# Rebuilding the prologue of a fused layer-norm, attention and GLU kernel: V projected early, statistics over two engines, the reciprocal root on GpSimd

## Chip, cores, metric

One core of a Trainium2 chip. The metric is the device time of one execution in microseconds (us). A program is run several times, in turn with the kernel before on the same chip; medians are quoted, and ratios with a 95% interval. **A ratio is the mean time of one kernel's fast runs over that of the other's of the same rounds**, so it is not quite the ratio of the medians. "Faster" needs 2%.

Engines: PE (matmuls; PEld is its loading of weights), ACT (ScalarE), DVE (VectorE), POOL (GpSimd), SP (issues DMAs). In the traces below ACT, DVE and POOL each work through one queue in order, which will matter (in run u, POOL's copy that waited 7.76 us for a load held up all that stood behind it). An eviction copies a result out of PSUM, where matmuls leave it in banks. The granted clock is the share of full speed that PE was given (1.00 is full). In a chain of waits, "issue" is time in which an engine waited for nothing that the profile shows, and POOLq is POOL's sequencer. `L260` is line 260 of the kernel; the two kernels' line numbers differ.

## The reference, cut to what matters

```python
x: [1, 2048, 640] bf16;  wqkv: [640, 1920];  wo: [640, 640];  w_gate, w_up: [640, 1728];  w_down: [1728, 640]
xn = (x - mean(x)) / sqrt(var(x) + 1e-5)                 # over the 640 columns
q, k, v = split of xn @ wqkv;   32 heads of 20
s = concat_heads(softmax(q @ k.T * 20**-0.5) @ v) @ wo
g = silu((sigmoid(xn @ w_gate) * (xn @ w_up)) @ w_down)
out = x + s * g
```

## The kernel before

Three stages. The **prologue** normalizes x in four quarters of 512 rows (4 tiles of 128 rows each), transposes it, and projects K (all quarters) and q (the first 512) of heads 0-3. It ends with the first score matmul, because the scores need q, which needs a bound made from the maximum over all of K. The **loop** runs attention and the GLU interleaved. Its order of issue on PE, ACT and DVE is made at build time by a small list scheduler with a model of durations and some tuned constants. Most exponentials are ACT's (from PSUM); for up to four key tiles in each block of 512 queries they are DVE's: an eviction to integers for each head, then four passes over the tile, after which PE needs four matmuls a head instead of one. The **tail** projects the last outputs.

The prologue (statistics, root, scaling, transposes, K):

```python
for c in range(NQC):                                  # 4 quarters
    for i in range(4):                                # DVE: statistics of 128 rows
        for h in range(2):
            nc.vector.bn_stats(out=stats[:, h, :], in_=xt[:, i, h * HD:(h + 1) * HD])
        nc.vector.bn_aggr(out=mv[:, i, :], in_=stats)
    nc.scalar.activation(out=rstd, in_=mv[:, :, 1:2], func=ACT.Sqrt, bias=eps_t, scale=1.0)
    if c == NQC - 1:
        exp_act(eps_t, eps_t)                         # loads the table of Exp
    nc.vector.reciprocal(out=rstd, in_=rstd)
    nc.vector.scalar_tensor_tensor(out=nb, in0=mv[:, :, 0:1], scalar=-1.0, in1=rstd, ...)
    for i in range(4):                                # DVE: the scalings
        nc.vector.tensor_scalar(out=xn[:, i, :], in0=xt[:, i, :], scalar1=rstd[:, i, :], scalar2=nb[:, i, :], ...)
    for kd in range(KD):                              # PE transposes, ACT copies
        ... nc.tensor.transpose(...) ; nc.scalar.copy(out=xnT[:, kd, c * 512:(c + 1) * 512], in_=tp)
    k_mm(psk, 0, c); k_evac(psk, 0, c, on_act=True)
    k_max(0, c)                                       # DVE, reads the evicted K
    # c == 0: q_mm, q_abs
q_bound(psq, 0, aq0); q_evac(psq, qts[0])
# ... (POOL fills constants before all this; cut)
```

The loop (V of heads 0-7 is an item of it; the q of later units takes an Abs on ACT; the last GLU tile has 64 of 128 columns):

```python
URGENT, ROUNDS, HOLD, SLACK, LEAD, LAG, D_LAST, D_LAST_END = 0.15, 4, 0.0, 0.1, 20.0, -5.0, 20, 0
items = [mk_v(0, t, 0.0) for t in VT]
def ab(): aqs[(u, c)] = q_abs(st["ps"])               # ACT Abs from PSUM, 16 times
# mk_gu: 5 matmuls for gate, 5 for up, for every tile, the half one too
# ...
```

The prologue's instructions are ordered by the compiler's tile scheduler, not in program order, on every engine.

## Time and profile before

| kernel before | us |
|---|---|
| median of its 3 first runs (883.49 to 885.87) | 885.81 |
| the profiled run | 879.89, span 878.0 |
| prologue, to the first score matmul | 36.5 |
| first score to the end of the last exponential | 818.3 |

The page's busy times, share of the span, and numbers of instructions:

```profile
PE 825.9 (94%) x7177; PEld 292.7 (33%) x7232; DVE 712.7 (81%) x1234; ACT 823.1 (94%) x1064; POOL 92.1 (10%) x134
```

By windows, prologue and loop (each engine's busy us and, in brackets, its instructions; then granted PE clock, DMA share, GB/s):

```profile
core 0: us, PE busy (x) PEld busy (x) DVE busy (x) ACT busy (x) POOL busy (x), PEclk, DMA share, GB/s
0.00:36.47 36.47, 16.58 (x106) 8.97 (x109) 25.85 (x80) 16.97 (x32) 8.96 (x30) 0.95 0.57 156
36.47:854.80 818.33, 792.31 (x6962) 275.86 (x7018) 676.55 (x1135) 806.13 (x1032) 74.39 (x94) 1.00 0.24 66
```

In the prologue DVE is the busiest engine; in the loop ACT is busy 98.5% and PE 96.8% of the time.

Some pieces of the chain of waits through the prologue (start, length, what):

```profile
11.43 1.41 DVE xn L261 x4
14.35 2.73 DVE xn L261 x4
...
30.27 2.55 ACT xnT L269 x5
...
32.86 0.39 PE psk L144
...
33.27 0.70 ACT kT_81 L152
...
33.99 0.70 DVE mk_223 L160
```

DVE's scalings are the first link; the last quarter's copies, K, eviction and maximum are the last. The second quarter's four scalings took twice the first's; POOL was filling constants then.

### The profile page before, as it was taken

The page shows a single profiled execution, that of the slowest core. Times are in us where ns is not written, and L with a number is a line of the kernel's source. Part 1 is how long each engine was busy: PE and PEld are TensorE (multiplying, and loading weights), DVE is VectorE, ACT ScalarE, POOL GpSimd, SP SyncE. Part 2 cuts the span into 40 slices and gives each one's busy share as a digit, 9 for nine tenths or more (in the row PEclk, how much of TensorE's full clock was granted, in tenths as well). Part 3 has the DMA queues.
Part 4 walks back from the last instruction along what each step waited for, and adds up shares of the span by engine and source line. Part 5 has one row for each costly group of instructions (what it writes and reads, how often), then busy time and mean ns, then how long its engine had stood idle before and what let it go on. Part 6 is the DMA issues. An engine that isn't in the chain of part 4 may idle for free.

```text
span 878.0 us, 18830 instructions
## 1 busy us (share of the span) xinstructions
PE 825.9 (94%) x7177; PEld 292.7 (33%) x7232; DVE 712.7 (81%) x1234; ACT 823.1 (94%) x1064; POOL 92.1 (10%) x134
## 2 busy tenths in 40 slices
PE   3699999999999999999999999999999999988897
PEld 2333223333333323333333333334333233322233
DVE  8558988988877798678878878989888868988884
ACT  4699999999999999999999999999999999999990
POOL 4010000111000000010000000002000000002233
PEclk9899999999999999999999999999999999999998
DMA  7401212122222132212113222211122211241332
GB/s 208 144 11 47 58 46 66 50 59 59 71 67 77 35 82 79 59 47 75 41 48 82 71 78 72 82 51 48 44 71 72 66 43 47 75 133 54 102 105 98
DMA packets 90361, 61.98 MB, mean 71 GB/s; under 512 B 32024, under 2 KB 83784, under 8 KB 90272
## 3 DMA queue, kind: packets, MB, share of 16 engines
q1 hardware_dynamic: 88832, 59.15, 24.2%
q10 hardware_dynamic: 1440, 1.64, 0.6%
q8 instruction: 56, 0.92, 0.4%
q14 instruction: 33, 0.27, 0.1%
HBM read 45.91 MB, written 12.39 MB: 66 GB/s over the span
## 4 chain that ended last, share of the span: by engine, by line
PE 41%; ACT 39%; DVE 12%; issue 7%; DMA 1%; POOLq 0%; SPq 0%; DVEq 0%; POOL 0%; ACTq 0%
PE oacc L780 11%; PE scA_449 L740 6%; PE scA_448 L740 6%; DVE pb L825 4%; PE bk_452 L538 4%; DVE iv L1044 4%; PE bk_451 L561 2%; PE bk_450 L538 2%; ACT tnh L87 2%; PE bk_452 L402 1%; DVE stats L249 1%; PE bk_450 L561 1%; PE bk_452 L561 1%; PE bk_451 L538 1%; ACT aq L174 1%
## 5 line engine op out<-in xcount | busy, mean ns | idle before, releaser
L825 DVE TENSOR_SCALAR pb<-iv 128x2048 int16<-128x2048 int16 x424 | 291.7, 708 | 2.5
L1044 DVE TENSOR_SCALAR iv<-bk_452 128x512 int16<-128x512 f32 x165 | 112.8, 684 | 35.5 <-PE bk_452 L740 35.0
L1044 DVE TENSOR_SCALAR iv<-bk_450 128x512 int16<-128x512 f32 x138 | 94.1, 682 | 31.2 <-PE bk_450 L740 30.9
L810 POOL TENSOR_TENSOR on_bf<-on,rl 128x512 bf16<-128x512 f32 x30 | 40.1, 1337 | 608.5 <-DMA rl<-rd 431.1
L1044 DVE TENSOR_SCALAR iv<-bk_451 128x512 int16<-128x512 f32 x121 | 82.5, 682 | 23.5 <-PE bk_451 L740 23.4
L538 PE MATMUL bk_452<-xnT,wgu 128*128 128x512 bf16 (+1 forms) x274 | 80.7, 383 | 1.7 <-issue 1.0
L740 PEld LDWEIGHTS <-kT_81 32*128 32x128 bf16 x1024 | 38.2, 91 | 131.0 <-issue 127.8
L780 PE MATMUL oacc<-pb,vs_86 128*21 128x512 bf16 x648 | 80.3, 382 | 1.3 <-DVE pb L825 1.0
L740 PEld LDWEIGHTS <-kT_82 32*128 32x128 bf16 x1024 | 39.8, 91 | 117.2 <-issue 109.2
L780 PE MATMUL oacc<-pb,vs_85 128*21 128x512 bf16 x624 | 70.6, 381 | 0.5 <-issue 0.3
L538 PEld LDWEIGHTS <-wgu 128*128 128x128 bf16 (+1 forms) x560 | 43.0, 98 | 70.0 <-issue 44.6
L561 PEld LDWEIGHTS <-hT 128*128 128x128 bf16 x448 | 35.4, 97 | 43.7 <-issue 34.2
L780 PEld LDWEIGHTS <-v_84 128*21 128x21 bf16 x1024 | 30.5, 90 | 45.5 <-issue 36.3
L780 PEld LDWEIGHTS <-v_83 128*21 128x21 bf16 x1024 | 29.1, 90 | 43.4 <-issue 33.4
L538 PE MATMUL bk_450<-xnT,wgu 128*128 128x512 bf16 x140 | 40.5, 382 | 0.8 <-issue 0.6
L780 PE MATMUL oacc<-pb,v_84 128*21 128x512 bf16 x216 | 33.7, 382 | 1.7 <-DVE pb L825 1.5
L561 PE MATMUL bk_451<-wd,hT 128*128 128x320 bf16 (+1 forms) x168 | 33.4, 303 | 0.0
L538 PE MATMUL bk_451<-xnT,wgu 128*128 128x512 bf16 (+1 forms) x99 | 29.2, 383 | 1.1 <-issue 0.6
L780 PE MATMUL oacc<-pb,v_83 128*21 128x512 bf16 x208 | 30.2, 383 | 0.0
L740 PE MATMUL scA_448<-q_94,kT_81 32*128 32x512 bf16 x134 | 27.3, 386 | 1.4 <-DVE q_94 L181 0.8
L780 PEld LDWEIGHTS <-vs_86 128*21 128x21 bf16 x648 | 21.5, 91 | 21.3 <-issue 14.4
L740 PE MATMUL scA_449<-q_95,kT_82 32*128 32x512 bf16 x133 | 26.4, 383 | 1.3 <-ACT pt_5196 L87 0.5
(1834 smaller groups left out, 2377.8 us busy)
## 6 DMA issues: line engine op xcount, KB each, us to landing
wgu<-in_B_w_gate_dram SPq DMA_DIRECT2D x24, 320.0 KB
wgu<-in_B_w_up_dram SPq DMA_DIRECT2D x24, 320.0 KB
rl<-rd SPq DMA_DIRECT2D x120, 64.0 KB
gq_dram<-gqs SPq DMA_DIRECT2D x32, 160.0 KB
ob<-gq_dram SPq DMA_DIRECT2D x12, 320.0 KB
wd<-in_B_w_down_dram SPq DMA_DIRECT2D x1, 2080.0 KB
oU<-on_bf SPq DMA_DIRECT2D x104, 20.0 KB
ob<-in_A_x_dram SPq DMA_DIRECT2D x12, 160.0 KB
```

What stands on the lines that cost most here:

```text
L87: return nc.scalar.add_instruction(mybir.InstActivation(func=func, name=nc.get_next_instruction_name(), engine=ENG.Activation, ins=[nc.sca ...
L174: nc.scalar.activation(out=aq, in_=ps, func=ACT.Abs)
L249: nc.vector.bn_stats(out=stats[:, h, :], in_=xt[:, i, h * HD:(h + 1) * HD])
L402: nc.tensor.matmul(st["ps"][0:UC, :], lhsT=wus[u][:, kd, i, :], rhs=xnT[:, kd, c * QC:(c + 1) * QC], start=(kd == 0), stop=(kd == KD - 1))
L538: nc.tensor.matmul(st[key][0:fs, :], lhsT=w[:, i, kd, ko * P:ko * P + fs], rhs=xnT[:, kd, c * QC:(c + 1) * QC], start=(kd == 0), stop=(kd ...
L561: nc.tensor.matmul(st["ps"][:, 0:HD], lhsT=hT[0:fsz[kf], kf, t4 * P:(t4 + 1) * P], rhs=wd[0:fsz[kf], kf, h * HD:(h + 1) * HD], start=(kf = ...
L740: nc.tensor.matmul(dst, lhsT=kTs[(b // NQC) % 2][32 * j:32 * j + 32, kt * P:(kt + 1) * P], rhs=qts[b % 3][32 * j:32 * j + 32, :], start=Tr ...
L780: nc.tensor.matmul(oacc[32 * j:32 * j + DH + 1, :], lhsT=lhsT, rhs=u["src"], start=first, stop=last, tile_position=(0, 32 * j), skip_group ...
L810: nc.gpsimd.tensor_tensor(out=on_bf, in0=on, in1=rl, op=ALU.mult)
L825: nc.vector.tensor_scalar(out=pb[:, k, :, :].bitcast(I16), in0=iv, scalar1=0.25, scalar2=cst, op0=ALU.mult, op1=ALU.add)
L1044: nc.vector.tensor_scalar(out=d["iv"][:, j, :], in0=bank[bk], scalar1=I_OFF, scalar2=I_LOW, op0=ALU.add, op1=ALU.max)
```

## The change

Its intent: shorten the prologue, use its idle PE for V of heads 0-7, and relieve ACT and PE in the loop.

```diff
-URGENT, ROUNDS, HOLD, ... D_LAST, D_LAST_END = 0.15, 4, 0.0, 0.1, 20.0, -5.0, 20, 0
+URGENT, ROUNDS, HOLD, ... D_LAST, D_LAST_END = 0.1, 4, 0.3, 0.1, 20.0, -5.0, 16, 8
@@ prologue (cut to its core) @@
+def stats_act(c, i):                       # one tile of four in each quarter: ACT
+    nc.scalar.activation(out=sq, in_=xts[c][:, i, :], func=ACT.Copy, scale=1.0 / D, accum_out=mvs[c][:, i, 0:1])
+    nc.scalar.mul(out=nm, in_=mvs[c][:, i, 0:1], mul=-root)
+    nc.scalar.activation(out=sq, in_=xts[c][:, i, :], func=ACT.Square, bias=nm, scale=root, accum_out=mvs[c][:, i, 1:2])
-    nc.scalar.activation(out=rstd, in_=mv[:, :, 1:2], func=ACT.Sqrt, bias=eps_t, scale=1.0)
-    nc.vector.reciprocal(out=rstd, in_=rstd)
+def rstd_of(c):                            # POOL: (var + eps) ** -0.5
+    nc.gpsimd.tensor_scalar(out=rstd, in0=mvs[c][:, :, 1:2], scalar1=1e-5, scalar2=0.0, op0=ALU.add, op1=ALU.add)
+    nc.gpsimd.tensor_tensor(out=rstd, in0=rstd, in1=mhalf, op=ALU.pow)
-    k_max(0, c)
+    k_max(0, c, psk)                       # from PSUM; one K bank instead of two
+    project_v(c)                           # 20 matmuls, ACT evicts
+exp_act(eps_t, eps_t)                      # the only table load, at the start
+for i in range(3): stats_dve(0, i)
+stats_act(0, 3)
+for c in range(NQC):
+    rstd_of(c)
+    if c == 0: spread_wst(0, wst0)
+    if c == 1: constants()                 # POOL's fillings, before: ahead of the loop
+    if c == 3: more_constants()
+    if c + 1 < NQC:
+        stats_act(c + 1, 3)
+        stats_dve(c + 1, 0)
+    scale(c)                               # nb, scalings, transposes; in the last quarter DVE makes 2 of 5 copies
+    if c + 1 < NQC:
+        for i in (1, 2): stats_dve(c + 1, i)
+    project_k(c); project_v(c)
@@ loop @@
-items = [mk_v(0, t, 0.0) for t in VT]
+items = []
-            aqs[(u, c)] = q_abs(st["ps"])                                   # ACT
+            nc.vector.scalar_tensor_tensor(out=aqs[(u, c)][0:UC, :], in0=st["q"], scalar=-1.0,
+                                           in1=st["q"], op0=ALU.mult, op1=ALU.max)
+        # last GLU tile: 64 gate and 64 up columns side by side in one tile, 5 matmuls instead of 10
```

The loads of x are also spread over two queues by tile instead of by quarter, and the loop's order of issue is made anew.

More of the change, by code (lines that the diff above doesn't have):

```diff
@@ L30 @@
 UC = UH * DH
-URGENT, ROUNDS, HOLD, SLACK, LEAD, LAG, D_LAST, D_LAST_END = 0.15, 4, 0.0, 0.1, 20.0, -5.0, 20, 0
+URGENT, ROUNDS, HOLD, SLACK, LEAD, LAG, D_LAST, D_LAST_END = 0.1, 4, 0.3, 0.1, 20.0, -5.0, 16, 8
 D_ORD, M_ORD, WAIT3, FALL = 0, 1, 0.0, 1
@@ L116 @@
     eps_t = const.tile([P, 1], FP32, name="eps_t")
+    mhalf = const.tile([P, 4, 1], FP32, name="mhalf")
     qts = [persist.tile([P, QC], BF16, name=f"q{i}") for i in range(3)]
@@ L124, with load_wst @@
     wqkv_v = A_wqkv.rearrange("(kd p) (t c) -> p kd t c", p=P, t=3)
-    def load_wqk(g):
+    def load_wst(g):
         st = wk.tile([P, KD, 2, GC], BF16, tag="wst", bufs=1, name="wst")
@@ L129, in load_wqk, with spread_wst @@
             nc.sync.dma_start(out=st[:, :, t, :], in_=wqkv_v[:, :, t, g * GC:(g + 1) * GC])
+        return st
+    def spread_wst(g, st):
         nc.gpsimd.tensor_copy(out=wqks[g % 2][:, :, :, 1:1 + DH],
@@ L154, in k_evac, with k_max @@
             nc.vector.tensor_scalar(out=dst, in0=ps, scalar1=ones_r[:, 0:1], scalar2=None, op0=ALU.add)
-    def k_max(g, c):
+    def k_max(g, c, src=None):
         if not mk_n.setdefault(g, []):
@@ L159, in k_max @@
         mk_n[g].append(c)
-        nc.vector.tensor_reduce(out=mks[g][:, c:c + 1], in_=kTs[g % 2][:, c * 512:(c + 1) * 512],
+        nc.vector.tensor_reduce(out=mks[g][:, c:c + 1], in_=kTs[g % 2][:, c * 512:(c + 1) * 512] if src is None else src,
                                 axis=AXISX, op=ALU.max, apply_absolute_value=True)
@@ L187, in v_mm, with v_evac @@
                                  rhs=w[:, kd, :], start=(kd == 0), stop=(kd == KD - 1))
-    def v_evac(ps, pr, tts):
+    def v_evac(ps, pr, tts, copy=None):
+        copy = copy or nc.vector.tensor_copy
         n = len(tts)
         src = ps[:, 0:n * 2 * GC].rearrange("p (t h e) -> p t h e", t=n, e=DH)
-        nc.vector.tensor_copy(out=vts[pr % 2][:, tts[0]:tts[0] + n, :, 1:1 + DH], in_=src)
+        copy(out=vts[pr % 2][:, tts[0]:tts[0] + n, :, 1:1 + DH], in_=src)
         for i, tt in enumerate(tts):
@@ L195, in v_evac @@
                 vf = wk.tile([P, 2 * GC], FP32, tag="vf", bufs=1, name="vf")
-                nc.vector.tensor_copy(out=vf, in_=ps[:, i * 2 * GC:(i + 1) * 2 * GC])
+                copy(out=vf, in_=ps[:, i * 2 * GC:(i + 1) * 2 * GC])
                 for b in range(1, NB):
@@ L206 @@
             tc.tile_pool(name="psP", bufs=2, space=bass.MemoryType.PSUM) as psP:
-        xts = []
+        xts = [lp.tile([P, 4, D], BF16, tag="xt", bufs=4, name="xt") for _ in range(NQC)]
         for c in range(NQC):
-            xt = lp.tile([P, 4, D], BF16, tag="xt", bufs=4, name="xt")
-            eng = nc.sync if c % 2 == 0 else nc.scalar
             for i in range(4):
-                r0 = (4 * c + i) * P
-                eng.dma_start(out=xt[:, i, :], in_=x2[r0:r0 + P, :])
-            xts.append(xt)
-        nc.vector.memset(eps_t, 1e-5)
-        make_identity(nc, ident)
-        nc.gpsimd.tensor_copy(out=ident_f, in_=ident)
-        for w in wqks:
-            nc.gpsimd.memset(w.rearrange("p a j e -> p (a j e)"), 0.0)
-        load_wqk(0)
-        wv0 = load_wv(0)
+                eng = nc.sync if i % 2 == 0 else nc.scalar
+                eng.dma_start(out=xts[c][:, i, :], in_=x2[(4 * c + i) * P:(4 * c + i + 1) * P, :])
+            if c == 0:
+                wst0 = load_wst(0)
+        wv0 = load_wv(0)
+        nc.vector.memset(eps_t, 0.0)
+        nc.vector.memset(mhalf, -0.5)
+        make_identity(nc, ident)
+        nc.gpsimd.memset(wqks[0].rearrange("p a j e -> p (a j e)"), 0.0)
         nc.gpsimd.memset(ones_r, 0.0)
@@ L224 @@
             nc.gpsimd.memset(ones_r[32 * j:32 * j + 1, :], 1.0)
-        nc.gpsimd.memset(esum, -1.0)
-        esum_v = esum.rearrange("p (j i) -> p j i", i=32)
-        nc.gpsimd.affine_select(out=esum_v, in_=esum_v, compare_op=ALU.is_ge, fill=0.0,
-                                base=0, pattern=[[-32, GH], [-P, 32]], channel_multiplier=1)
-        nc.gpsimd.affine_select(out=esum_v, in_=esum_v, compare_op=ALU.is_ge, fill=0.0,
-                                base=31, pattern=[[32, GH], [P, 32]], channel_multiplier=-1)
@@ L231 @@
-        nc.gpsimd.memset(esum_u, -1.0)
-        nc.gpsimd.affine_select(out=esum_u, in_=esum_u, compare_op=ALU.is_ge, fill=0.0,
-                                base=0, pattern=[[-DH, UH]], channel_multiplier=1)
-        nc.gpsimd.affine_select(out=esum_u, in_=esum_u, compare_op=ALU.is_ge, fill=0.0,
-                                base=DH - 1, pattern=[[DH, UH]], channel_multiplier=-1)
-        for i in range(2):
-            nc.gpsimd.memset(vts[i].rearrange("p t h c -> p (t h) c")[:, :, 0:1], 1.0)
-            if ND:
-                for b in range(1, NB):
-                    nc.gpsimd.memset(vss[i][:, :, b - 1, :, 0:1], ALPHA[b])
@@ L242, with constants @@
-        aq0 = psq = None
-        for c in range(NQC):
-            xt = xts[c]
-            mv = lp.tile([P, 4, 2], FP32, tag="mv", name="mv")
-            for i in range(4):
-                stats = lp.tile([P, 2, nc.vector.BN_STATS_DIM], FP32, tag="stats", bufs=3, name="stats")
-                for h in range(2):
-                    nc.vector.bn_stats(out=stats[:, h, :], in_=xt[:, i, h * HD:(h + 1) * HD])
-                nc.vector.bn_aggr(out=mv[:, i, :], in_=stats)
-            rstd = lp.tile([P, 4, 1], FP32, tag="rstd", name="rstd")
-            nc.scalar.activation(out=rstd, in_=mv[:, :, 1:2], func=ACT.Sqrt, bias=eps_t, scale=1.0)
-            if c == NQC - 1:
-                exp_act(eps_t, eps_t)
-            nc.vector.reciprocal(out=rstd, in_=rstd)
+        def constants():
+            nc.gpsimd.memset(esum, -1.0)
+            esum_v = esum.rearrange("p (j i) -> p j i", i=32)
+            nc.gpsimd.affine_select(out=esum_v, in_=esum_v, compare_op=ALU.is_ge, fill=0.0,
+                                    base=0, pattern=[[-32, GH], [-P, 32]], channel_multiplier=1)
+            nc.gpsimd.affine_select(out=esum_v, in_=esum_v, compare_op=ALU.is_ge, fill=0.0,
+                                    base=31, pattern=[[32, GH], [P, 32]], channel_multiplier=-1)
+            for b in range(1, NB):
+                nc.gpsimd.memset(vss[0][:, :, b - 1, :, 0:1], ALPHA[b])
+            nc.gpsimd.memset(vts[0].rearrange("p t h c -> p (t h) c")[:, :, 0:1], 1.0)
@@ new lines, in more_constants @@
+        def more_constants():
+            nc.gpsimd.memset(esum_u, -1.0)
+            nc.gpsimd.affine_select(out=esum_u, in_=esum_u, compare_op=ALU.is_ge, fill=0.0,
+                                    base=0, pattern=[[-DH, UH]], channel_multiplier=1)
+            nc.gpsimd.affine_select(out=esum_u, in_=esum_u, compare_op=ALU.is_ge, fill=0.0,
+                                    base=DH - 1, pattern=[[DH, UH]], channel_multiplier=-1)
+            nc.gpsimd.tensor_copy(out=ident_f, in_=ident)
+            nc.gpsimd.memset(wqks[1].rearrange("p a j e -> p (a j e)"), 0.0)
+            nc.gpsimd.memset(vts[1].rearrange("p t h c -> p (t h) c")[:, :, 0:1], 1.0)
+            for b in range(1, NB):
+                nc.gpsimd.memset(vss[1][:, :, b - 1, :, 0:1], ALPHA[b])
@@ new lines, with stats_dve @@
+        mvs = [lp.tile([P, 4, 2], FP32, tag="mv", bufs=NQC, name="mv") for _ in range(NQC)]
+        rstds, nbs = {}, {}
+        root = float(D) ** -0.5
+        def stats_dve(c, i):
+            stats = lp.tile([P, 2, nc.vector.BN_STATS_DIM], FP32, tag="stats", bufs=3, name="stats")
+            for h in range(2):
+                nc.vector.bn_stats(out=stats[:, h, :], in_=xts[c][:, i, h * HD:(h + 1) * HD])
+            nc.vector.bn_aggr(out=mvs[c][:, i, :], in_=stats)
+        def stats_act(c, i):
+            sq = lp.tile([P, D], BF16, tag="sq", bufs=2, name="sq")
+            nm = lp.tile([P, 1], FP32, tag="nm", bufs=2, name="nm")
+            nc.scalar.activation(out=sq, in_=xts[c][:, i, :], func=ACT.Copy, scale=1.0 / D,
+                                 accum_out=mvs[c][:, i, 0:1])
+            nc.scalar.mul(out=nm, in_=mvs[c][:, i, 0:1], mul=-root)
+            nc.scalar.activation(out=sq, in_=xts[c][:, i, :], func=ACT.Square, bias=nm, scale=root,
+                                 accum_out=mvs[c][:, i, 1:2])
@@ L256, with scale @@
+        def rstd_of(c):
+            rstd = lp.tile([P, 4, 1], FP32, tag="rstd", name="rstd")
+            nc.gpsimd.tensor_scalar(out=rstd, in0=mvs[c][:, :, 1:2], scalar1=1e-5, scalar2=0.0,
+                                    op0=ALU.add, op1=ALU.add)
+            nc.gpsimd.tensor_tensor(out=rstd, in0=rstd, in1=mhalf, op=ALU.pow)
+            rstds[c] = rstd
+        def scale(c):
             nb = lp.tile([P, 4, 1], FP32, tag="nb", name="nb")
-            nc.vector.scalar_tensor_tensor(out=nb, in0=mv[:, :, 0:1], scalar=-1.0, in1=rstd,
+            nc.vector.scalar_tensor_tensor(out=nb, in0=mvs[c][:, :, 0:1], scalar=-1.0, in1=rstds[c],
@@ L260 @@
             for i in range(4):
-                nc.vector.tensor_scalar(out=xn[:, i, :], in0=xt[:, i, :], scalar1=rstd[:, i, :],
+                nc.vector.tensor_scalar(out=xn[:, i, :], in0=xts[c][:, i, :], scalar1=rstds[c][:, i, :],
                                         scalar2=nb[:, i, :], op0=ALU.mult, op1=ALU.add)
@@ L268, with project_k, project_v @@
                 dst = xnT[:, kd, c * 512:(c + 1) * 512]
-                nc.scalar.copy(out=dst, in_=tp)
-            psk = psP.tile([P, 512], FP32, tag="pk", bufs=2, name="psk")
+                if c == NQC - 1 and kd % 2 == 1:
+                    nc.vector.tensor_copy(out=dst, in_=tp)
+                else:
+                    nc.scalar.copy(out=dst, in_=tp)
+        def project_k(c):
+            psk = psP.tile([P, 512], FP32, tag="pk", bufs=1, name="psk")
             k_mm(psk, 0, c)
             k_evac(psk, 0, c, on_act=True)
-            k_max(0, c)
-            if c == 0:
-                psq = psP.tile([P, 512], FP32, tag="pq", bufs=1, name="psq")
+            k_max(0, c, psk)
+        def project_v(c):
+            for i in (0, 2):
+                tts = [4 * c + i, 4 * c + i + 1]
+                psv = psP.tile([P, 512], FP32, tag="pv", bufs=2, name="psv")
+                v_mm(psv, wv0, tts)
+                v_evac(psv, 0, tts, nc.scalar.copy)
+        exp_act(eps_t, eps_t)
+        psq = psP.tile([P, 512], FP32, tag="pq", bufs=1, name="psq")
+        for i in range(3):
+            stats_dve(0, i)
+        stats_act(0, 3)
+        for c in range(NQC):
+            rstd_of(c)
+            if c == 0:
+                spread_wst(0, wst0)
+            if c == 1:
+                constants()
+            if c == 3:
+                more_constants()
+            if c + 1 < NQC:
[3 more added lines that the diff above has]
+            if c + 1 < NQC:
+                for i in (1, 2):
+                    stats_dve(c + 1, i)
+            project_k(c)
+            project_v(c)
+            if c == 0:
                 q_mm(psq, 0, 0)
@@ L299 @@
     wgu_tiles = {}
+    NK2 = (NFT + 1) // 2
+    assert NFT % 2 == 0 and fsz[-1] == P // 2
     def load_wgu(c, k2):
@@ L306, in load_wgu @@
         nc.sync.dma_start(out=w[:, 1, :, 0:fw], in_=B_w_up[:, f0:f0 + fw].rearrange("(kd p) f -> p kd f", p=P))
+        if k2 == NK2 - 1:
+            ls = fsz[-1]
+            nc.sync.dma_start(out=w[:, 0, :, fw:fw + ls],
+                              in_=B_w_up[:, F - ls:F].rearrange("(kd p) f -> p kd f", p=P))
         wgu_tiles[(c, k2)] = w
-    NK2 = (NFT + 1) // 2
     out_tiles = {}
@@ L443, in ab @@
         def ab():
-            aqs[(u, c)] = q_abs(st["ps"])
+            aqs[(u, c)] = wk.tile([P, QC], BF16, tag="aq", bufs=4, name="aq")
+            nc.vector.scalar_tensor_tensor(out=aqs[(u, c)][0:UC, :], in0=st["q"], scalar=-1.0, in1=st["q"],
+                                           op0=ALU.mult, op1=ALU.max)
         def ev():
-            q = wk.tile([P, QC], BF16, tag="ku", bufs=2, name="qu")[0:UC, :]
-            nc.vector.tensor_scalar_mul(out=q, in0=st["ps"][0:UC, :], scalar1=qscale)
-            nc.sync.dma_start(out=qD[u][:, c * QC:(c + 1) * QC], in_=q)
+            st["q"] = wk.tile([P, QC], BF16, tag="ku", bufs=2, name="qu")[0:UC, :]
+            nc.vector.tensor_scalar_mul(out=st["q"], in0=st["ps"][0:UC, :], scalar1=qscale)
+            nc.sync.dma_start(out=qD[u][:, c * QC:(c + 1) * QC], in_=st["q"])
         return Item([("PE", alloc, [(T_MM, lambda kd=kd: u_mm(st, u, 0, c, kd)) for kd in range(KD)]),
-                     ("ACT", 0.48, ab, "", mark("aq", u, c)),
-                     ("DVE", 0.60, ev, "free", mark("qD", u, c))], at, pre=[("bD", u - 1)] if u else [])
+                     ("DVE", 0.60, ev, "free", mark("qD", u, c)),
+                     ("DVE", 0.60, ab, "", mark("aq", u, c))], at, pre=[("bD", u - 1)] if u else [])
     def mk_bu(u, at):
@@ L466, in ev @@
             bt = wk.tile([P, QC], BF16, tag="ku", bufs=2, name="bt")
-            nc.vector.tensor_scalar_mul(out=bt, in0=st["ps"], scalar1=qscale)
+            nc.vector.tensor_copy(out=bt, in_=st["ps"])
             for c in range(NQC):
@@ L547, in ev, with mm2, th2, ev2 @@
                                            in1=st["u"][0:fs, :], op0=ALU.add, op1=ALU.mult)
+        def mm2(kd):
+            nc.tensor.matmul(st["g"], lhsT=wgu_tiles[(c, k2)][:, 0, kd, P:2 * P],
+                             rhs=xnT[:, kd, c * QC:(c + 1) * QC], start=(kd == 0), stop=(kd == KD - 1))
+        def th2():
+            st["t"] = w2.tile([P, QC], BF16, tag="tnh", bufs=2, name="tnh")
+            act_imm(st["t"][fs:P, :], st["g"][0:fs, :], ACT.Tanh, 0.5)
+        def ev2():
+            nc.vector.scalar_tensor_tensor(out=hT[0:fs, kf, :], in0=st["t"][fs:P, :], scalar=1.0,
+                                           in1=st["g"][fs:P, :], op0=ALU.add, op1=ALU.mult)
+        if fs < P:
+            return [Item([("PE", alloc0, [(T_MM, lambda kd=kd: mm2(kd)) for kd in range(KD)]),
+                          ("ACT", 0.48, th2), ("DVE", 0.60, ev2, "free", mark("h", c, kf))], at)]
         return [Item([("PE", alloc0, [(T_MM, lambda kd=kd: mm("g", 0, kd)) for kd in range(KD)]),
@@ L673 @@
                 glu.append(lambda at, c=c, t4=t4, h=h: [mk_down(c, t4, h, at)])
-    items = [mk_v(0, t, 0.0) for t in VT]
+    for t in range(TT):
+        v_at[(0, t)] = 0.0
+    items = []
     for b in range(NBLK):
@@ L962 @@
                 if c == 0 and g + 1 < PG:
-                    load_wqk(g + 1)
+                    spread_wst(g + 1, load_wst(g + 1))
                 if c == 0 and g + 1 < NG:
```

## The prediction

> What bounds the kernel now. The busy table shows PE 94%, ACT 94%, DVE 81%, POOL 10% of an 878.0 us span (timed median 885.81 us). By windows there are three stages. (1) Prologue, 0 to 36.5 us (first score matmul): PE 16.6 us busy, ACT 17.0, DVE 25.9. The chain of waits runs through the xt load, then DVE (statistics and scaling, nearly without a gap from 6.0 to 23.5 us), then ACT's sqrt, and from 30.3 to 36.5 us the last quarter's copies, K, its eviction, its maximum, q. (2) The attention and GLU loop, 36.5 to 853 us: ACT 804.4 of 816.5 us busy (98.5%), PE 790.5 (96.8%), DVE 674.8 (82.6%). ACT and PE are both full; the list of waits shows only stalls under 3.1 us. From 740 us on ACT is still at 99% while PE falls to 90%. (3) Tail, 853 to 878 us, untouched.
>
> What changes, costed.
> a) Loop, ACT: 16 of its 23 Abs go to DVE. Starts of successive ACT instructions give 0.47 us for one: ACT loses 7.5 us. DVE gets 16 operations, estimated like other 512-column DVE operations at 0.60 us: 9.6 us.
> b) Loop, PE: the merged last GLU tile takes 5 matmuls in place of 10, for 4 query chunks: 20 x 0.213 = 4.3 us less. V of heads 0-7 leaves the loop: 80 matmuls of 160 columns, 0.08 to 0.11 us each, 6.4 to 8.6 us. PE: -11 to -13 us. DVE also loses about 5 us of V evictions.
> c) Prologue: a quarter of DVE's 13.7 + 3.1 us of statistics goes to ACT: -4.2 us. ACT loses one table load (1.28 us in this trace; the Trainium skill, "ScalarE: Activation LUTs", What ACT_TABLE_LOAD costs, gives about 1283 ns, which agrees) but gains four Copy/Square pairs (1.6 to 2 us each, estimated from the 512-column copies at 0.5 us) and V evictions, about 1 us per quarter. So ACT becomes the prologue's limit: about 6 us per quarter from about 13 us on. Splitting the last copies and taking the K maximum from PSUM saves about 1.7 us of the last chain. Net: the loop starts 1 to 5 us earlier, estimate 2.5.
> d) The order of issue is made anew with other constants; a larger DVE share of the exponentials turns spare PE and DVE time into less ACT time (a key tile of four heads is 1.9 us of ACT).
>
> On the critical path: in the loop ACT's 7.5 us counts nearly whole, because PE is relieved as well; with a slightly larger DVE share 8 to 11 us. DVE's extra 5 us is off the path. Together 11 to 13 us: 1.4%. Predicted 873 us, from 866 to 880. Faster by over 2% (under 868.1 us): 0.2; within 2%: 0.78; slower: 0.02.
>
> What would show it. First score matmul at 32 to 35 us; ACT 23 us or more busy in the prologue; no V matmuls in the first 10 us of the loop; the loop 8 to 11 us shorter with ACT still near 98%; L1044 evictions 424 to 440; the tail still about 25 us.
>
> What would make it wrong. ACT's prologue work (after 6.8 us of issuing loads on its queue) delays the first xn and eats the gain. POOL operations block DVE: the second quarter's scalings took 2.82 us against 1.50 in the others while POOL was filling constants (the Trainium skill, "SBUF — State Buffer", Who interferes with whom, describes an exclusive shared port; the trace agrees in direction). Or the new issue order closes more of the stretch after 740 us than I count, and the gain passes 2%.

## The result

| | before | after |
|---|---|---|
| median of the timed runs, same chip, 4 each | 884.65 (883.09 to 885.87) | 880.45 (879.91 to 880.86) |
| ratio | | 0.9953 [0.9932, 0.9974] |
| profiled: span | 878.0 | 879.2 |
| first transpose | 11.8 | 16.6 |
| first score matmul | 36.5 | 42.6 |
| first score to the end of the last exponential | 818.3 | 814.2 |

The kernel takes 0.5% less time, not 1.4%; by the 2% rule it counts as the same. Before any experiment the profile shows where it went: the prologue did not become 2.5 us shorter, it became 6.1 *longer*. One trap: the only profile of before was a quick run (879.89, below all its timed ones), so its loop is not typical; the first experiment looks at that.

The page and the windows of the changed kernel:

```profile
PE 822.0 (93%) x7176; PEld 297.1 (34%) x7176; DVE 708.5 (81%) x1203; ACT 829.9 (94%) x1098; POOL 100.3 (11%) x142
```

```profile
core 0: us, PE busy (x) PEld busy (x) DVE busy (x) ACT busy (x) POOL busy (x), PEclk, DMA share, GB/s
0.00:42.56 42.56, 21.27 (x187) 15.03 (x188) 24.65 (x67) 24.08 (x57) 17.56 (x50) 0.96 0.46 128
42.56:856.80 814.24, 785.25 (x6897) 274.92 (x6897) 673.55 (x1117) 805.80 (x1041) 74.98 (x84) 1.00 0.25 68
```

No engine is full in the prologue (24.7 of 42.6 us at most): it waits. ACT's busy time in the loop is 805.8 us, and was 806.1: nothing came off ACT there.

Pieces of the chain of waits at the start of the changed kernel:

```profile
7.87 0.49 DVE stats L258
8.36 0.12 DVE mv L259
...
8.52 2.76 issue
...
11.33 0.23 POOL rstd L272
11.56 0.80 POOL wqk_87 L134
...
12.86 1.04 POOL rstd L274
13.90 0.22 POOL rstd L272
14.12 0.14 POOL esum L229
14.27 1.02 POOL rstd L274
...
15.31 0.16 DVE nb L279
15.48 0.12 DVE mv L259
15.60 5.81 DVE xn L283 x8
```

POOL's first rstd starts at 11.33 us; the list of waits names what it waited for, and who waits for POOL in turn:

```profile
POOL rstd L272 <- ACT sq L267: 8.8, 1, 8.8
DVE nb L279 <- POOL rstd L274: 5.2, 4, 1.5
```

(engine, line, releaser: us in total, times, longest). Three things follow on one another: ACT (busy issuing loads until 8.6 us, then running two quarters' statistics interleaved), POOL (whose queue holds the power behind ACT, and the filling of constants behind the power), DVE (whose queue has the small operation `nb` of the *second* quarter ahead of the *first* quarter's scalings). And the eight scalings then take 5.8 us, where four had taken 1.41. POOL's timeline in that window (start, length, instruction):

```profile
15.23 0.52 POOL L236 MEMSET vs_85<- 128x32 bf16 x3
15.40 0.92 POOL L237 MEMSET v_83<- 128x128 bf16 x1
15.91 0.76 POOL L231 TENSOR_SCALAR_AFFINE_SELECT esum<-esum 128x128 bf16<-128x128 bf16 x1
...
17.57 1.16 POOL L246 MEMSET wqk_88<- 128x1280 bf16 x1
...
18.90 0.67 POOL L247 MEMSET v_84<- 128x128 bf16 x1
```

It is the filling of constants, moved by the change into the middle of the scalings. So far all of this is a reading. The experiments test it.

### The profile page after: what moved, and what is told of

It reads as the page before. It is cut to its first block, busy times and chain, and to the rows that moved or that the text cites. A ratio compares the mean times of both kernels' runs of the same rounds, so it can differ in the third digit from the quotient of the medians.

```text
span 879.2 us, 18755 instructions
## 1 busy us (share of the span) xinstructions
PE 822.0 (93%) x7176; PEld 297.1 (34%) x7176; DVE 708.5 (81%) x1203; ACT 829.9 (94%) x1098; POOL 100.3 (11%) x142
## 4 chain that ended last, share of the span: by engine, by line
ACT 42%; PE 35%; DVE 13%; issue 8%; DMA 1%; POOL 1%; POOLq 0%; DVEq 0%; ACTq 0%
PE oacc L860 9%; DVE pb L905 5%; PE scA_571 L820 5%; PE scA_570 L820 5%; DVE iv L1124 4%; PE bk_574 L601 4%; ACT tnh L87 2%; PE bk_572 L463 1%; PE bk_574 L639 1%; PE bk_574 L463 1%; PE bk_572 L601 1%; DVE xn L283 1%; PE bk_573 L601 1%; PE bk_573 L639 1%; DMA xt<-in_A_x_dram 1%
## 5 line engine op out<-in xcount | busy, mean ns | idle before, releaser
L905 DVE TENSOR_SCALAR pb<-iv 128x2048 int16<-128x2048 int16 x412 | 287.9, 723 | 2.7
L1124 DVE TENSOR_SCALAR iv<-bk_574 128x512 int16<-128x512 f32 x147 | 100.6, 685 | 37.9 <-PE bk_574 L820 37.2
L1124 DVE TENSOR_SCALAR iv<-bk_573 128x512 int16<-128x512 f32 x147 | 100.4, 683 | 31.6 <-PE bk_573 L820 31.4
L1124 DVE TENSOR_SCALAR iv<-bk_572 128x512 int16<-128x512 f32 x118 | 80.6, 683 | 20.0 <-PE bk_572 L820 19.5
L601 PE MATMUL bk_574<-xnT,wgu 128*128 128x512 bf16 x305 | 84.0, 383 | 0.1
L820 PEld LDWEIGHTS <-kT_81 32*128 32x128 bf16 x1024 | 39.0, 91 | 127.8 <-issue 124.5
L820 PEld LDWEIGHTS <-kT_82 32*128 32x128 bf16 x1024 | 41.5, 91 | 118.7 <-issue 109.3
L860 PE MATMUL oacc<-pb,vs_86 128*21 128x512 bf16 x648 | 76.4, 383 | 2.8 <-DVE pb L905 2.4
L860 PE MATMUL oacc<-pb,vs_85 128*21 128x512 bf16 x588 | 71.0, 381 | 0.0
L601 PEld LDWEIGHTS <-wgu 128*128 128x128 bf16 x520 | 40.2, 98 | 64.4 <-issue 38.4
L860 PEld LDWEIGHTS <-v_84 128*21 128x21 bf16 x1024 | 31.2, 91 | 48.9 <-issue 39.1
L860 PEld LDWEIGHTS <-v_83 128*21 128x21 bf16 x1024 | 30.4, 91 | 44.8 <-issue 35.8
L639 PE MATMUL bk_574<-wd,hT 128*128 128x320 bf16 x238 | 44.7, 302 | 0.2 <-DVE iv L1124 0.2
L609 DVE SCALAR_TENSOR_TENSOR hT<-tnh,bk_574 128x512 bf16<-128x512 bf16 x34 | 23.2, 684 | 15.4 <-PE bk_574 L601 14.5
L860 PE MATMUL oacc<-pb,v_84 128*21 128x512 bf16 x216 | 32.0, 386 | 0.6 <-DVE on L873 0.5
L601 PE MATMUL bk_573<-xnT,wgu 128*128 128x512 bf16 x110 | 31.0, 383 | 0.3 <-DVE iv L1124 0.3
L860 PEld LDWEIGHTS <-vs_86 128*21 128x21 bf16 x648 | 21.8, 91 | 23.1 <-issue 15.3
L601 PE MATMUL bk_572<-xnT,wgu 128*128 128x512 bf16 x105 | 29.4, 382 | 0.1
L860 PE MATMUL oacc<-pb,v_83 128*21 128x512 bf16 x196 | 29.2, 382 | 0.0
L820 PE MATMUL scA_570<-q_96,kT_82 32*128 32x512 bf16 x124 | 25.3, 390 | 2.7 <-ACT pt_10608 L87 1.0
```

What stands on the lines that cost most here:

```text
L601: nc.tensor.matmul(st[key][0:fs, :], lhsT=w[:, i, kd, ko * P:ko * P + fs], rhs=xnT[:, kd, c * QC:(c + 1) * QC], start=(kd == 0), stop=(kd ...
L609: nc.vector.scalar_tensor_tensor(out=hT[0:fs, kf, :], in0=st["t"][0:fs, :], scalar=1.0, in1=st["u"][0:fs, :], op0=ALU.add, op1=ALU.mult)
L639: nc.tensor.matmul(st["ps"][:, 0:HD], lhsT=hT[0:fsz[kf], kf, t4 * P:(t4 + 1) * P], rhs=wd[0:fsz[kf], kf, h * HD:(h + 1) * HD], start=(kf = ...
L820: nc.tensor.matmul(dst, lhsT=kTs[(b // NQC) % 2][32 * j:32 * j + 32, kt * P:(kt + 1) * P], rhs=qts[b % 3][32 * j:32 * j + 32, :], start=Tr ...
L860: nc.tensor.matmul(oacc[32 * j:32 * j + DH + 1, :], lhsT=lhsT, rhs=u["src"], start=first, stop=last, tile_position=(0, 32 * j), skip_group ...
L905: nc.vector.tensor_scalar(out=pb[:, k, :, :].bitcast(I16), in0=iv, scalar1=0.25, scalar2=cst, op0=ALU.mult, op1=ALU.add)
```

## Experiments

Unless said otherwise each variant gave the reference's result. "First score" is the start of the first score matmul in the variant's profile. Two looks at one and the same kernel differed in it by up to 1.8 us (e_pool_power_only and e_again below), so smaller differences are not read.

### Two looks at the kernel before

No edit.

> The kernel before, unchanged, once more: what differs between two looks at one program. The first profile of it was a run of 879.9 us while its timed runs had a median of 884.65. Theory A (that look was a lucky one, and the loop is what varies): the first score matmul again at 36.5 us within 0.5, and the time from it to the end of the last exponential about 823 us where the first look had 818.3. Theory B (the look was typical and the timed runs carry something outside the span): the loop is 818 again and the timed ratio to itself is 1.000 within 0.002.

Measured: 884.62 us, ratio to itself 1.0020 [0.9995, 1.0045]; first score 36.9; first score to the end of the last exponential 823.3 us, as theory A said. The two looks differ at the start of the loop. First look, by windows of 5 us:

```profile
35.00:40.00 5.00, 3.40 (x25) 2.02 (x26) 2.75 (x6) 2.62 (x4) 0.00 (x0) 0.72 1.07 355
40.00:45.00 5.00, 5.00 (x54) 2.35 (x51) 3.71 (x7) 4.78 (x6) 0.99 (x3) 0.93 0.43 146
45.00:50.00 5.00, 4.66 (x57) 2.06 (x50) 4.92 (x10) 5.00 (x7) 0.99 (x3) 1.00 0.01 3
```

Second look:

```profile
35.00:40.00 5.00, 3.21 (x22) 1.75 (x22) 2.95 (x7) 2.43 (x3) 0.00 (x0) 0.60 1.07 357
40.00:45.00 5.00, 5.00 (x33) 2.38 (x34) 1.88 (x4) 3.42 (x4) 0.98 (x3) 0.50 0.52 173
45.00:50.00 5.00, 5.00 (x35) 1.50 (x36) 3.79 (x7) 3.54 (x5) 0.00 (x0) 0.50 0.00 0
```

The column after POOL's is the granted clock: 0.50 for ten microseconds in the second look, with PE full throughout. Summing (1 - clock) x time from 35 to 60 us gives 8.6 us lost in the second look and 1.8 in the first. The changed kernel loses 0.3 there (and 3.4 us later, between 769.6 and 776.4 us, where neither look at before loses any). So a typical run of before has a loop some 5 us longer than the profile I predicted from, and the changed kernel's loop is 4.1 us shorter than the quick look and 9.1 us shorter than this one. That V's matmuls in the prologue keep the clock up is plausible, but no run isolates it: in the 25 us after the first score the traces with V in the loop (before twice, and b below) lose 1.7 to 8.1 us, those with V in the prologue and a record of the clock 0 to 3.3. That stays open.

### Which half of the change: prologue or loop

`b_new_loop_only`: the new constants, GLU tile and Abs; the old prologue, V in the loop. `c_new_prologue_only`: the reverse.

> New constants, merged GLU tile and the units' Abs on DVE, but the old prologue, V of heads 0-7 back in the loop. First score matmul at 36.5 us (old value) under every theory. My theory (the new prologue lost about 6 us and the loop gained about 10): the loop keeps most of its gain less what V costs, 3 to 6 us under before, total 879 to 882. Rival (the loop hardly gained, the prologue is harmless): total 883 or more.

> The new prologue with V projected there, and the old loop (old constants, GLU tile not merged, Abs on ACT). First score matmul at 42.6 us, as in the changed kernel. My theory: 6 us lost there, about 4 to 6 us won in the loop by V's absence: total within 3 us of before (882 to 888). Rival (the prologue is harmless): 878 or less.

Measured: b 881.05 us, ratio 0.9982 [0.9951, 1.0014], first score 37.0. c 889.70 us, ratio 1.0076 [1.0053, 1.0100], first score 41.8. The new prologue alone makes the kernel 0.8% slower. The new loop alone hardly helps without V's departure. In c my theory held for the prologue (+5.4 us) but not for the loop: V's absence won nothing with the old constants, and the granted clock fell between 740 and 840 us (8.5 us lost in the sense above, none in before), so c does not price V. The parts do not simply add.

### The statistics path, undone

```diff
-            nc.gpsimd.tensor_scalar(out=rstd, ...); nc.gpsimd.tensor_tensor(..., op=ALU.pow)
+            nc.scalar.activation(out=rstd, in_=mvs[c][:, :, 1:2], func=ACT.Sqrt, bias=eps_t, scale=1.0)
+            if c == NQC - 1: exp_act(eps_t, eps_t)
+            nc.vector.reciprocal(out=rstd, in_=rstd)
-        stats_act(0, 3) ... stats_act(c + 1, 3)
+        stats_dve(0, 3) ... stats_dve(c + 1, 3)
```

> The changed kernel with one part of the prologue undone: all statistics on DVE and rstd by Sqrt on ACT and reciprocal on DVE, as before; V stays in the prologue. Theory S (statistics on ACT and the power on POOL delay the first scaling): the first transpose moves from 16.6 back to about 12 us and the first score matmul from 42.6 to about 38.5; total 876 to 877. Rival V (PE and ACT work of the V projection, and the single K bank, set the pace): first transpose earlier, but the first score matmul still at 41 us or later.

Measured: **874.16 us**, ratio 0.9907 [0.9879, 0.9934]; first transpose 11.8, first score 35.8 (theory S had said about 38.5). V stayed in the prologue, with its single K bank, and cost nothing visible. The statistics path holds all of the loss: 6.8 us of first score. Rival V falls, and so does the new spreading of the loads, which d keeps. This kernel's loop is the changed kernel's, instruction for instruction in its order of issue. Its total is close to the 873 us that I had predicted for the change, but not for the reason given there: its loop starts only 0.7 us earlier than before's, not 2.5.

### Which half of the statistics path

`e_pool_power_only`: all statistics on DVE, the power stays on POOL. `f_act_stats_only`: a quarter of the statistics on ACT, the root as before.

> The changed kernel with the statistics all on DVE but the power of -0.5 still on POOL: one half of the statistics change alone. If POOL's part (0.23 + 1.04 us and its turn in POOL's queue, per quarter) is what delays the start: first transpose at 14.5 us or later, first score at 39 us or later. If the statistics on ACT are: first transpose near 12 to 13 us, first score 35 to 37 us, total 872 to 875.

> The other half alone: a quarter of the statistics on ACT as in the changed kernel, rstd by ACT's Sqrt and DVE's reciprocal. If ACT's statistics delay the start: first transpose 15 us or later and first score 39 to 42.5 us. If POOL was to blame: first transpose near 12 us, first score 35 to 37 us.

Measured: e **872.17 us**, ratio 0.9865 [0.9822, 0.9908], first transpose 12.0, first score 34.6. f: fast runs 876.8 to 879.6 us, ratio 0.9923 [0.9877, 0.9969]; its profiled run was a slow one, 1365.33 us, with score matmuls at a mean of 534 ns (386 in the repetition). Why is not known: its trace holds no record of the clock. It was repeated:

> f_act_stats_only again, for a profile in the fast state (in its first one PE ran at about half speed for the whole run). First transpose at 14.0 us again; first score between d_old_statistics (35.8) and the changed kernel (42.6), about 38 to 40 us, by its total of 876.8 to 879.6.

f2: 874.87 us (one run, state unknown), first transpose 14.5, first score 37.6. That makes a square of first scores:

| first score, us | root on ACT and DVE | power on POOL |
|---|---|---|
| statistics all on DVE | 35.8 (d) | 34.6 and 36.5 (e, e_again) |
| a quarter of them on ACT | 37.6 (f2) | 42.6 (the change) |

Each half alone costs at most about 2 us; together they cost about 7. I had expected one of them to be guilty. Neither is; what they do *together* is. The reading, which the next section tests, is that they meet in POOL's queue: with both, POOL's power waits for ACT, and the filling of constants, queued behind the power, slides into all eight of DVE's first scalings. In f2 POOL has no power to wait for, fills from 7 to 13 us, and the scalings (from 14.0 us) take 1.50 us for four.

### POOL's filling

First attempt: in the changed kernel, write the filling after the scalings.

```diff
-            if c == 1: constants()
-            if c == 3: more_constants()
             project_k(c)
+            if c == 0: constants()
+            if c == NQC - 1: more_constants()
```

> The changed kernel with POOL's filling of constants moved behind the scalings (the small ones after the first quarter's K, the rest after the last quarter's). In the changed kernel the first eight scalings took 5.89 us while POOL filled constants, where four alone take 1.48. If POOL's filling holds DVE up: eight scalings in about 3 us, the first score 2 to 3 us earlier than 42.6. If not: still near 5.9 us and 42.6.

Measured: 878.61 us, ratio 0.9940 [0.9899, 0.9981], first score 40.7. Nearly a miss: the tile scheduler made its own order again, and much of the filling still ran between 13.6 and 19.8 us, under the scalings of the first quarter (1.85 us for four) and of the second (2.84). Writing it later did not make it later. Writing it *first* did make it earlier:

```diff
+        constants()
+        more_constants()
         exp_act(eps_t, eps_t)
```

This was tried on three kernels. `n_first_quarter_dve` is the change with only the first quarter's fourth tile moved back to DVE; `r_best` is n with the filling early; `s_change_early_fill` is the change itself with the filling early and nothing else.

> The changed kernel with one row tile's statistics moved back: the fourth tile of the first quarter on DVE, those of the other three quarters still on ACT. If the loss is the wait of the first quarter for ACT (which issues loads until 8.6 us and then runs two quarters' statistics interleaved): first transpose about 12 us as in e_pool_power_only, first score 33 to 36 us, total 871 to 874. If ACT's statistics in general overload the prologue: first transpose near 12 but first score 38 us or later.

> The same, and POOL's constants filled before its first rstd instead of between the quarters' rstd: the version meant to be best. If POOL's filling is what holds up DVE's first scalings (2.5 us in e_pool_power_only against 1.5 undisturbed) and the first rstd, the first score comes 1 to 2 us earlier than in n_first_quarter_dve; total 870 to 872. If not, equal to it.

> The changed kernel with one thing moved: POOL fills its constants before its first rstd, not between the quarters'. If POOL's filling is the larger part of the loss: the first eight scalings in about 2.9 us in place of 5.9, first score at 37.5 to 39 us in place of 42.6, total 874 to 877. If ACT's statistics are the larger part: first score still at 40.5 us or later.

> All statistics on DVE, the power on POOL, POOL's filling early. If ACT's share of the statistics costs by itself: first transpose near 11 us and first score 33 to 34 us, 2 to 3 us before r_best (35.9), total 869 to 872, the best so far. If ACT's share is harmless without POOL's filling: first score 35.5 us or later, no better than r_best.

| first score, us (ratio to before) | filling between the powers | filling first |
|---|---|---|
| four tiles' statistics on ACT | 42.6 (0.9953, the change) | 37.5 (0.9922, s) |
| three | 40.5 (0.9946, n) | 35.9 (0.9890, r) |
| none | 34.6, 36.5 (0.9865, 0.9877; e, e_again) | 36.1 (0.9883, t) |

n has a median of 879.61 us and r of 873.64 on one chip, s 876.36 and t 873.62 on another. DVE's first scalings in the changed kernel and in s:

```profile
15.52 5.89 DVE L283 TENSOR_SCALAR xn<-xt,rstd,nb 128x640 bf16<-128x640 bf16 x8
14.79 2.89 DVE L283 TENSOR_SCALAR xn<-xt,rstd,nb 128x640 bf16<-128x640 bf16 x8
```

DVE's timeline in n:

```profile
11.28 0.15 DVE L279 SCALAR_TENSOR_TENSOR nb<-mv,rstd 128x4 f32<-128x4 f32 x1
13.06 0.16 DVE L279 SCALAR_TENSOR_TENSOR nb<-mv,rstd 128x4 f32<-128x4 f32 x1 [1.51 <-POOL rstd L274]
13.14 6.02 DVE L283 TENSOR_SCALAR xn<-xt,rstd,nb 128x640 bf16<-128x640 bf16 x8
```

and in r:

```profile
13.14 0.15 DVE L279 SCALAR_TENSOR_TENSOR nb<-mv,rstd 128x4 f32<-128x4 f32 x1
13.64 0.16 DVE L279 SCALAR_TENSOR_TENSOR nb<-mv,rstd 128x4 f32<-128x4 f32 x1 [0.34 <-POOL rstd L274]
13.83 2.89 DVE L283 TENSOR_SCALAR xn<-xt,rstd,nb 128x640 bf16<-128x640 bf16 x8
```

The same eight scalings on the same data take 5.89 or 2.89 us, and 6.02 or 2.89; the kernels of a pair differ in where POOL fills. r's scalings even start 0.7 us later, and its first score comes 4.6 us earlier. The Trainium skill, "SBUF — State Buffer", *Who interferes with whom*, says that DVE in a 2-port mode and GpSimd share a port pair that one instruction holds for its whole length; the trace agrees: twice the time under filling, none of it recorded as a wait. (No run shows the mode that the scalings run in.) n's timeline also answers n's own expectation: the first `nb` was ready at 11.28 us, but DVE's queue had the second quarter's `nb` next, and that waited for ACT's statistics through POOL. So freeing the first quarter from ACT did not bring the first transpose to 12 us (14.3); my theory of that run fell.

The gain of moving the filling is 5.0 us of first score in the changed kernel, 4.6 in n and none where ACT has no statistics (t against e). In e the filling also runs under the first scalings, but only under four of them (2.48 us; the next four take 1.47), so about 1 us is lost; and t gives that back, because its queue puts both `nb` together and its scalings start at 12.98 us, not at 11.56.

Not all of the 5.0 us is in the scalings. When the eight end (21.41 us in the changed kernel, 17.68 in s) 3.7 us are there; of n's 4.6 us, 2.4 are (19.16 and 16.72). The rest comes later, and two things stand there in the changed kernel and in n, but not in s and r. PE waits for the one K bank, which DVE's late maximum still holds: 2.3 and 2.7 us, two waits each.

```profile
PE psk L148 <- DVE mk_232 L164: 2.3, 2, 1.5
```

And the granted clock is 0.50 for 3.4 us (32.3 to 35.7 us in the changed kernel, 30.1 to 33.5 in n), with PE in the chain of waits. So 5.0 us is the price of the filling with what followed from it; no run separates the share of the clock, at most half of 3.4 us. With the filling out of the way, statistics on ACT cost 1.4 us (s against t), which is within what two looks differ by, so whether ACT's share is harmful by itself is not resolved.

### Ordering DVE by hand

r's order still puts both `nb` together. So DVE's order in the prologue was fixed to program order, with each K maximum one quarter late; the rest as r. `e_again` ran beside it.

```diff
+        with tc.manual_schedule(engines={ENG.DVE}):
             for c in range(NQC): ...
                 scale(c)
+                if c > 0: k_max(0, c - 1, psks[c - 1])
```

> POOL's filling early, the first quarter's statistics all on DVE, a quarter of the other three on ACT, and DVE's order in the prologue fixed by hand: a quarter's scalings go ahead of the statistics of the quarter after next, the K maximum one quarter late. If the order of DVE's queue is what is left of the loss: first transpose at 10.5 to 12 us (14.3 in r_best), first score 32 to 34.5 us (35.9), total 868 to 872. If ACT or PE sets the pace of the quarters by now: first transpose earlier but first score 35 us or later, total as r_best and e_pool_power_only (872 to 874).

> e_pool_power_only once more, on the same chip as u_order_dve and at five rounds: 871 to 874, 0.985 to 0.989 of before; first score at 34.6 us.

Measured: u **881.42 us**, ratio 0.9952 [0.9923, 0.9982]; first transpose 11.1 as expected, first score 41.0: a plain failure. e_again 873.21, ratio 0.9877 [0.9846, 0.9909], first score 36.5. Why u failed, from its timelines. DVE:

```profile
20.29 0.16 DVE L280 SCALAR_TENSOR_TENSOR nb<-mv,rstd 128x4 f32<-128x4 f32 x1 [5.20 <-POOL rstd L275]
```

and POOL:

```profile
18.09 0.85 POOL L134 COPY wqk<-wst 128x800 bf16<-128x800 bf16 x1 [7.76 <-DMA wst<-in_A_wqkv_dram]
18.90 0.23 POOL L273 TENSOR_SCALAR rstd<-mv 128x4 f32<-128x4 f32 x1
```

The second quarter's rstd sat in POOL's queue behind a copy of the *next* group's weights, and that waited 7.76 us for a load. The same disease again, with another carrier. So u does not tell what DVE's order is worth: that stays untested.

### The loop's terms

`k_d_old_constants`: d with the old scheduling constants. `o_e_no_abs`, `o_e_no_glu`: e with the 16 Abs back on ACT, or with the last GLU tile not merged. Each makes a new order of issue, which no run can hold fixed.

> The kernel of d_old_statistics (874.2 us) with the old scheduling constants, so a new order of issue for the loop with 107 key tiles on DVE in place of 103. If my reading of the loop is right (ACT-bound, so a larger DVE share helps, 1.9 us per tile): 868 to 872. If PE binds (each tile on DVE costs PE twelve matmuls more): slower than d, 876 to 881.

> e_pool_power_only (872.2 us) with the units' 16 Abs back on ACT; the order of issue is made anew (108 key tiles on DVE). My prediction put 7.5 us on this step. Right: 876 to 880. If the loop's two full engines share the gain, or the order of issue gives it away: 873 to 875.

> e_pool_power_only with the last GLU tile not merged: 20 matmuls, 4.3 us of PE, back; the order of issue is made anew (101 key tiles on DVE). If PE binds the loop: 875 to 877. If ACT alone binds it: 871 to 873.

Measured: k 875.76 us, ratio 0.9904 [0.9867, 0.9941], against d's 0.9907: four key tiles more on DVE won nothing, neither what I expected (868 to 872) nor the loss that the rival expected. o_e_no_abs 876.71, ratio 0.9909 [0.9882, 0.9936]; o_e_no_glu 878.39, ratio 0.9939 [0.9905, 0.9972]. Against e (0.9865 and 0.9877) that is 0.3 to 0.4%, 3 to 4 us for the Abs, and 0.6 to 0.7%, 5 to 7 us for the GLU tile. These come from different calls, and the intervals overlap in part, so the sizes are rough. The Abs are worth about half of the 7.5 us that ACT spent on them; the GLU tile seems worth about its 4.3 us of PE or somewhat more. That fits a loop in which both engines bind, but does not prove it.

### Best version

e_pool_power_only: 872.17 and 873.21 us on two chips, 1.2 to 1.4% under before (0.9865 and 0.9877). It is under the changed kernel's 0.9953 with an interval that does not touch it. They were run at other times. r, t and d (0.9890, 0.9883, 0.9907) have intervals that overlap e's and are not told apart from it.

## Why the prediction was wrong

The step that failed is c): "Net: the loop starts 1 to 5 us earlier, estimate 2.5." It started 6.1 us later. That is a miss of 8.6 us; the predicted change of the total was -12.8 us (885.81 to 873), the measured one -4.2 (884.65 to 880.45): also 8.6 us. The rest of the sum came out about right in total, but partly by luck (the loop, below), and not in its parts.

- **What bounds it: right.** ACT and PE are both full in the loop (98.5% and 96.8%), DVE is the busiest in the prologue.
- **c), the prologue: wrong, in kind and not only in size.** The step was "So ACT becomes the prologue's limit: about 6 us per quarter". I added up busy time: 4.2 us off DVE, about 6 us per quarter on ACT. ACT was 24.1 us busy, as I said ("23 us or more"), but that is 24.1 of 42.6 us: it was no limit. The prologue is a chain of hand-overs. The change made it DVE to ACT to POOL to DVE, through queues that run in order, and the filling behind POOL's wait landed on DVE's scalings. s shows 5.0 us of it, with what followed, by moving the filling alone; the table of halves shows that ACT's statistics and POOL's power do it only together; e and d show the first score at 34.6 to 36.5 us without the pair, where I had said 32 to 35. I had named both dangers ("delays the first xn", "POOL operations block DVE") and given them no microseconds. The chain of before already had the price: 2.73 us against 1.41 for four scalings.
- **V and the single K bank: right.** V in the prologue cost nothing visible there (d), though in the changed kernel the one bank did make PE wait for a late DVE. d against b, 874.16 to 881.05 us on one chip, prices V together with the shorter last chain, and with the clock (from the first score on b's profile loses 5.7 us to it and d's 3.4), at about 7 us; my figure for V was 6.4 to 8.6 us of PE.
- **a), Abs off ACT "counts nearly whole": wrong in the trace.** ACT's busy time in the loop stayed at 806, because the new order gave DVE 412 evictions and not 424 to 440: three key tiles of four heads went back to ACT, 5.7 us at my own 1.9 us a tile. (That leaves 1.5 of the 7.5 us unaccounted for.) The worth of the step is 3 to 4 us.
- **b), GLU tile: right or a little small**, 4.3 us predicted, 5 to 7 measured, roughly.
- **d), a larger DVE share: wrong.** The share fell, and raising it (k) won nothing, since each tile on DVE costs PE twelve matmuls more.
- **The loop 8 to 11 us shorter: right against the second look at before (9.1), wrong against the profile I used (4.1).** The 9.1 is luck. From the first score to the last exponential the clock cost 8.1 us in the second look, 1.7 in the first and 3.4 in the changed kernel. Taken out at full price, 815.3 and 816.6 us of before stand against 810.8: an estimate of 4.5 to 5.8 us for the loop's gain at an equal clock, about half of what I predicted. The clock, which I did not foresee, stood in for the rest.
- **The tail: about right**, 23 us before (854.8 to 878.0) and 22 after (856.8 to 879.2), where I had said about 25.

The evictions in the groups of the changed kernel, by the bank that they read (line, engine, operation, shapes, count; busy us, mean ns; idle before them), for the count 147 + 147 + 118 = 412:

```profile
L1124 DVE TENSOR_SCALAR iv<-bk_574 128x512 int16<-128x512 f32 x147 | 100.6, 685 | 37.9 <-PE bk_574 L820 37.2
L1124 DVE TENSOR_SCALAR iv<-bk_573 128x512 int16<-128x512 f32 x147 | 100.4, 683 | 31.6 <-PE bk_573 L820 31.4
L1124 DVE TENSOR_SCALAR iv<-bk_572 128x512 int16<-128x512 f32 x118 | 80.6, 683 | 20.0 <-PE bk_572 L820 19.5
```

Left open: what holds the clock at half at the start of the loop in some runs, and late in the prologue of the changed kernel; whether statistics on ACT cost anything once POOL is out of the way; and the separate worth of each loop term under one fixed order of issue.

## What to carry to other kernels

When work moves to another engine in a start-up chain, do not subtract its busy time; list what stands ahead of it in the new engine's queue, and what stands behind it and will now run later. A wait put into such a queue moved everything behind it here, and work that was harmless (filling constants) can land where it collides. And before pricing a change of under 1%, profile the kernel before more than once: here one look was 5 us quicker than another.

## What the Trainium skill lacked or had wrong

- "ScalarE: Activation LUTs", *What ACT_TABLE_LOAD costs*: no price for an accumulator output. Each one in the changed kernel's prologue is followed by a separate read of the accumulator of 0.19 us (eight of them). Its figure of about 93 ns more for a pointer operand is borne out: 812 ns for Square with a tile as bias, 724 ns for Copy without one, both on 640 columns.
- No page that I found has the cost of a power on GpSimd: 1.04 us for 128x4 values, besides 0.23 us for the addition before it.
- "SBUF — State Buffer", *Who interferes with whom*: the lock is right, but its price should stand there: eight scalings of 128x640 in 6.02 us with POOL filling and 2.89 us without, and the loss shows up as longer DVE instructions, not as a wait.
- "TensorE: Matmul & The Clock Gate", *What's actually happening*: it has the clock rise after about 3.4 us of sustained work. In a second look at the kernel before the granted clock stayed at 0.50 from 40 to 50 us while PE was busy 10.0 of 10.0 us (by the profile's model of PE). The section gives no such exception; *Seeing it yourself* on the same page does warn that clock records can be unreliable and that a low clock has been seen to stick.
